# A last layer taken as two passes over all tokens, each with half of its inner width

## The chip, the cores and the metric

The kernel runs on one core of one Trainium2 chip. The metric is the device time of one execution in microseconds (us), as the median of several runs. The core has five engines with their own instruction queues: PE (TensorE, the matmuls; PEld is its weight load), DVE (VectorE), ACT (ScalarE), POOL (GpSimd) and SP (SyncE, which here only issues DMAs). Each engine works its queue in the order of the program; semaphores tie the engines together.

## The reference

Three stages over 3072 tokens of width 512. Inputs are float64 where the kernel converts them (the last layer's weights), the results float32.

```python
attn = softmax(mask(q @ k.T / 8)) @ v              # 4 batches, 8 heads, 768 tokens, window 128, 4 sinks
x    = rows of tokens, heads side by side           # (3072, 512)
# mixture of experts: each token goes to one of 8 experts
e    = argmax(x @ w_gate + modality_bias[modality])
x    = gate_weight * (relu(x @ w1[e]) @ w2[e])      # inner width 1024
# last layer, all tokens
h    = x @ w_in                                     # (3072, 2048)
out  = (h * sigmoid(1.702 * h)) @ w_out             # (3072, 512)
```

## The kernel before

Every float32 product is made of three products of parts: a value is split into a high part (rounded by ScalarE) and what is left (`exact`, line 1189: one ACT copy, then one subtraction on DVE or POOL), and high*high, low*high and high*low are summed in PSUM.

**Attention** (`attention`) is a hand-made schedule of steps; the change leaves it as it is. Tokens are then sorted by expert into slots of 128. Two slots of one expert make a **pair** (256 tokens); an odd last slot of an expert stands **alone**. This run has 12 pairs (the code for pairs 8 and up stands in nested conditions, `more_pairs`, line 1497) and 3 slots alone (`more_alone`, line 1569).

**A pair** (`pair`, line 1460) goes over the 8 chunks `f` of an expert's inner width. For each chunk PE does `first` (line 1248: 12 matmuls of 256 columns, line 1231) and, two chunks behind (`LAG = 2`), `second` (line 1444, `down_pair`: 12 matmuls, line 1246). Between them stands the relu and split of a chunk: ACT makes the high part (line 1254), DVE the low part (line 1257, tile `h`). In chunk 3 PE also transposes the next pair's tokens (line 1202). Beside this run: the gathers of tokens (POOL queue), the stores of the pair's result y with its token numbers to DRAM (SP queue, `columns`, lines 1302 and 1303), and, where a pair's expert differs from the one before, the load of its weights (16 DMAs of 256 KB in two-chunk portions, `others`, line 1435) and a pair later their split (ACT and DVE, 8 times).

**Conversion of the last layer's weights.** Beside the pairs, the last layer's weights come from float64 to float32. The work is cut in **units** (`convert`, `converted`, `stored`, lines 1401 to 1426): a unit is half a chunk of 128 of the last layer's inner width, of `w_in` (even) or of `w_out` (odd), 512 KB in DRAM. There are 32. `cload` (line 1387) brings a unit into one of two buffers `cd`; `convert` is 4 DVE operations (lines 1404 to 1407), `converted` 3 on DVE (lines 1413 to 1415) and a multiplication on POOL (line 1416), `stored` writes the unit away and issues the load of the unit after the next into the buffer that it frees. For the first 16 units `stored` makes the exact parts in place, in the tiles `wb` (two POOL operations, lines 1422 and 1423); for the last 16 there is no place beside the experts' weights, so it stores float32 values to DRAM (`wd`, line 1425, POOL's DMA queue). `units` (line 1489) says which units belong to which pair (`FIRST, SLOPE = 1, 3.2`: some 3.2 a pair), and `pair` spreads their three steps over its 8 chunks, in the program order of DVE: a `convert` whose load has not landed holds up whatever DVE has to do after it.

**The last layer** (from line 1587). The upper half of the weights is loaded from `wd` to the tiles `raw` (8 DMAs, line 1589) and split during the first group into `wa`, which held the experts' weights (`split(f)`, line 1621). Then, for each of 6 groups of 512 tokens, all 16 chunks: `up` (12 matmuls of 512 columns, line 1231), `act` (line 1599: ACT sigmoid, DVE product, ACT high part, DVE low part), and one chunk behind `down` (12 matmuls, line 1238). The next group's tokens are loaded to `cd` (`x2load`, line 1515) and split in the group's last chunk (`msplit`, line 1546: 4 times ACT and DVE). At a group's end `row_out` (line 1605) copies four PSUM tiles out, on DVE and ACT in turns, and POOL scatters their rows to the output (line 1611).

Of the kernel before, what the change touches and what calls it, by code (L numbers as in the profile page):

```python
# [19 lines left out]
NT = S // P            # token tiles of a batch  # L20
T = B * NT             # token tiles
E = 8
DM = H * D
XW = 72                # columns of a head in a row of x: 64 of x, 8 of its logits
KB = P + 4             # a block of keys and the sinks behind it
# [3 lines left out]
# when every kind of the attention's work is issued, in steps of a pair of heads behind its own  # L29
# [5 lines left out]
OPEN = dict(split1=2.908, x0=3.935, split0=4.324, x1=5.361, split2=5.435, split3=6.448, first0=6.794, first1=8.702, split4=13.836)     # steps behind the scores' last at which the first pair's beginnings are  # L35
MORE = 83.434, 0.509, 92.568, 1.089      # the step at which the search for the first pair starts, and its pace; those of its weights


def attention(tc, cst, late, first, spare, q, k, v, wg, xd, then, pick, at_tile, more, opening):
    """Sliding-window attention with sinks; x rows to xd, every tile's logits handed to then().  # L40

    Where the banded path doesn't hold, no rows are written and the logits are zero. The first two
    tiles and the first sinks are in `first`; at_tile holds what else to issue at a tile, `more` at a step.
    `opening` takes turns behind the last scores. `late` holds what the last tiles need longest.
    """
    nc = tc.nc
    ident = cst["ident"]
    with ExitStack() as ctx:
# [12 lines left out]
        def build_back():  # L61
            """Identity and the gate's weights, by head."""
            nc.gpsimd.memset(btw, 0.0)
            nc.gpsimd.tensor_scalar(out=wgs, in0=wgs, scalar1=cst["banded"], scalar2=None, op0=ALU.mult)
            nc.gpsimd.tensor_copy(identr, ident)
            for a in range(2):
                r = slice(64 * a, 64 * a + 64)
                for c in range(4):
                    nc.gpsimd.tensor_copy(btw[r, c, a, 0:64], ident[r, r])
                nc.gpsimd.tensor_copy(btw[r, :, a, 64:72], wgs[r])  # L70

        def build_heads():
            """Rows (part, head, sink) that belong to a head."""
# [11 lines left out]
        # values by head, with nothing beside them; those of a batch's last tile lie across, head beside head  # L85
# [4 lines left out]
        def alone(t):  # L90
            """A batch's last tile, whose own keys are for no other: but the last of all."""
            return t % NT == NT - 1 and t < T - 1

# [5 lines left out]
        # transposed probabilities: of key tile j, the halves are its two query tiles by parity  # L99
# [4 lines left out]
        # what only the scores need  # L104
# [4 lines left out]
        # a batch's first keys lie in the first block of the upper rows and in the second of the lower, with nothing beside them  # L109
# [25 lines left out]
        def load_gate():  # L135
            """The gate's weights of every row's head."""
# [13 lines left out]
        def split_sinks(b):  # L150
            """The sinks' values and logits in exact parts, by head."""
# [52 lines left out]
        def keys(t):  # L204
            """Rows and columns of a tile of keys."""
# [12 lines left out]
        def ksinks():  # L218
            """The sinks' keys behind every block."""
# [10 lines left out]
        def scores(t, c):  # L230
            """A pair of heads, one on the upper rows of the array and one on the lower."""
# [38 lines left out]
        def where(t, kk):  # L270
            """Which half of a bank the probabilities of key tile t - 1 + kk are in: by their places."""
# [51 lines left out]
        def zero(t, g):  # L323
            """The sums of query tile t start from nothing."""
            nc.scalar.activation(out=ops[g][:, :, t % 2, :], in_=zs.unsqueeze(2).broadcast_to([P, 2, P]), func=AF.Copy)

        def pv(t, c):
            """Probabilities times values: key tile t-1 for query tiles t-1, t; at a batch's last tile its own keys too."""
# [13 lines left out]
        def move(t, g):  # L342
            """The lower rows' sums to the other tile's place, which is free by now."""
# [3 lines left out]
        def own(t, g):  # L347
            """Its own keys, for both heads at once: each head's sums are right at one of the two places."""
# [17 lines left out]
        def back(t, g):  # L366
            """Back to tokens by rows, with the logits."""
# [18 lines left out]
        def norm(t, g):  # L386
            """Divided by the sums of the softmax."""
# [39 lines left out]
        # every kind of work: what a unit of it is (a step, half a tile, a tile), and when it is issued, by steps after the unit's own  # L427
# [69 lines left out]
def sink_rows(nc, vs, v, b):  # L497
    """A batch's values of the sinks, on rows (head, sink)."""
# [4 lines left out]
WARM = 13              # products of nothing before the branch, behind the first keys, and at the first steps  # L503
# [4 lines left out]
def warm(tc, cst, spare):  # L508
    """Products of nothing, which have TensorE's clock up by the first that count."""
# [14 lines left out]
def constants(tc, keep, pool, spare, n_sink, window):  # L524
    """Identity, whether the window and the sinks fit the banded path, and what builds its masks."""
    nc = tc.nc
    c = {}
    # the softmax's function, so that its table is there by then
# [9 lines left out]
    # query minus key in the tile's own block, and the key's number in its block  # L538
# [9 lines left out]
    # the banded path holds windows of 1 to P + 1 keys and up to four sinks  # L548
# [19 lines left out]
    def masks():  # L568
# [6 lines left out]
        # kept by the window in the own block and in the one before; kept as a sink in block 0  # L575
# [18 lines left out]
def general(tc, cst, q, k, v, wg, xd):  # L594
    """Attention over all keys, for any window and any number of sinks: x rows to xd, logits beside the bias."""
# [76 lines left out]
NP = 15                # pairs of slots of 128 tokens of one expert that any routing fits in  # L672
NP0 = 8                # pairs that any routing has
NQ = NP + 2
NC = T + E - 1         # slots that any routing fits in
NR = NC - 2            # without the first pair's
ROUND = 1.5 * 2.0 ** 30   # added and taken off again, it rounds to multiples of 128, and its double to those of 256
N0 = 2 * E             # tiles of which some expert has 256 tokens at least
EARLY = 20             # tiles whose experts are picked ahead of the others'


def route_bias(tc, cst, pool, spare, mid, mb):
    """The modality's bias of every token, and the logits of the general path's."""
# [28 lines left out]
def route_constants(tc, cst, pool):  # L712
    """Tiles of the routing's constants, and what fills them."""
# [9 lines left out]
    def fill():  # L723
        G.iota(t["rank"], pattern=[[0, T], [-1, E]], base=E, channel_multiplier=0, **big)       # 8 - e
        G.memset(t["tri"], 1.0)                                                                # q < p
# [4 lines left out]
        G.iota(t["pos"], pattern=[[2 * P, NQ]], base=-2 * P, channel_multiplier=0, **big)       # first places of pairs, behind the first pair  # L730
        G.iota(t["col"], pattern=[[P, 2 * NP - 2]], base=0, channel_multiplier=0, **big)
        G.iota(t["desc"], pattern=[[-P, E]], base=(E - 1) * P, channel_multiplier=0, **big)
        G.iota(t["tok"], pattern=[[P, T]], base=-T * P // 2, channel_multiplier=1, **big)       # the token, from the middle
# [4 lines left out]
def picker(tc, cst, pool):  # L738
    """Every token's expert, the first of the largest logits, as it comes."""
# [25 lines left out]
def opener(tc, cst, pool, perm, raw, gather, load):  # L765
    """The first pair: 256 tokens of the first expert that has as many in the first tiles. What to issue, in turns.

    Its tokens go to the first two columns; the others' routing counts them no more.
# [900 lines left out]
```

## Time and profile before

| | |
|---|---|
| median of 3 runs | 1184.71 us (1183.29 to 1187.19) |
| the profiled execution, first to last instruction (span) | 1182.5 us |
| attention, routing and the first pair | to about 285 us |
| pairs 1 to 11 | about 285 to 596 us |
| slots alone | 596 to 643 us |
| last layer | 643 us to the end |
| PE busy over the span | 93% |
| DVE, ACT, POOL busy | 50%, 38%, 25% |

The page gives no other time for the profiled execution than its span; it lies 2.2 us below the median of the runs. In the page's slices, the busy share of an engine is in tenths, and PEclk is the TensorE clock that was granted, in tenths of 2.4 GHz; its two levels are 1.2 and 2.4 GHz. A wait is put down to the engine or transfer that ended last before it.

### The profile page before, as it was taken

The page shows a single profiled execution, that of the slowest core. Times are in us where ns is not written, and L with a number is a line of the kernel's source. Part 1 is how long each engine was busy: PE and PEld are TensorE (multiplying, and loading weights), DVE is VectorE, ACT ScalarE, POOL GpSimd, SP SyncE. Part 2 cuts the span into 40 slices and gives each one's busy share as a digit, 9 for nine tenths or more (in the row PEclk, how much of TensorE's full clock was granted, in tenths as well). Part 3 has the DMA queues.
Part 4 walks back from the last instruction along what each step waited for, and adds up shares of the span by engine and source line. Part 5 has one row for each costly group of instructions (what it writes and reads, how often), then busy time and mean ns, then how long its engine had stood idle before and what let it go on. Part 6 is the DMA issues. An engine that isn't in the chain of part 4 may idle for free.

```text
span 1182.5 us, 19589 instructions
## 1 busy us (share of the span) xinstructions
PE 1105.4 (93%) x6925; PEld 976.3 (83%) x6925; DVE 591.4 (50%) x1419; ACT 451.3 (38%) x1098; POOL 290.1 (25%) x505
## 2 busy tenths in 40 slices
PE   6999999888999888998778999999999999999996
PEld 5888898788999888988677888888888888888885
DVE  4989898786655777666410533223223223223221
ACT  4999999653222332222121423223223223223221
POOL 5855463452443444323110001001001001001001
PEclk8999999898999898998978999999999999999998
DMA  6598889671778856566676201002002002000000
GB/s 114 102 126 116 112 114 103 97 149 55 111 120 121 222 101 141 118 144 186 175 181 195 49 1 62 10 1 72 1 1 72 1 1 72 1 1 36 1 1 36
DMA packets 164569, 98.07 MB, mean 83 GB/s; under 512 B 117616, under 2 KB 149360, under 8 KB 164432
## 3 DMA queue, kind: packets, MB, share of 16 engines
q1 hardware_dynamic: 158352, 76.75, 36.7%
q0 software_dynamic: 6080, 19.68, 4.9%
q8 instruction: 63, 1.03, 0.4%
q14 instruction: 74, 0.61, 0.2%
HBM read 71.22 MB, written 25.19 MB: 82 GB/s over the span
## 4 chain that ended last, share of the span: by engine, by line
issue 44%; DMA 10%; POOL 2%; PE 2%; DVE 1%; POOLq 0%; DVEq 0%; another core or an unknown queue 0%; ACT 0%; SPq 0%
DMA yb<-y 4%; DMA cd<-in_moe_w_in_dram 2%; DMA cd<-in_moe_w_out_dram 2%; POOL out_dram L1611 1%; DMA wd<-cw 1%; PE pa L1246 1%; DMA raw<-in_moe_w_dram 1%; POOL cw L1416 1%; PE pu L1231 0%; DVE ca L1404 0%; DVE cd L1405 0%; DVE cd L1406 0%; DVE ca L1407 0%; POOLq L1665 0%
## 5 line engine op out<-in xcount | busy, mean ns | idle before, releaser
L1602 DVE TENSOR_TENSOR s<-pu,s 128x512 f32<-128x512 f32 x96 | 66.4, 692 | 318.5 <-ACT s L1601 318.5
L1246 PE MATMUL pa<-h,wah 128*128 128x256 f32 x768 | 164.8, 297 | 30.3 <-DVE h L1257 19.3
L1231 PE MATMUL pu<-xh,wah 128*128 128x256 f32 (+1 forms) x576 | 187.5, 326 | 0.2 <-ACTq L1340 0.2
L1231 PE MATMUL pu<-xh,wal 128*128 128x256 f32 (+1 forms) x576 | 186.1, 323 | 0.5 <-DVEq L1340 0.5
L1231 PE MATMUL pu<-xl,wah 128*128 128x256 f32 (+1 forms) x576 | 185.9, 323 | 0.0
L1601 ACT ACTIVATE s<-pu 128x512 f32<-128x512 f32 x96 | 57.3, 597 | 306.0 <-PE pu L1231 306.0
L1246 PEld LDWEIGHTS pa<-h,wah 128*128 128x128 f32 x768 | 134.0, 203 | 33.2 <-DVE h L1257 21.4
L1611 POOL DMA_INDIRECT out_dram<-xg,oidx x12 | 11.9, 991 | 502.9 <-DVE xg L1610 501.0
L1231 PEld LDWEIGHTS pu<-xh,wal 128*128 128x128 f32 x576 | 112.4, 195 | 8.3 <-DVEq L1340 0.7
L1231 PEld LDWEIGHTS pu<-xh,wah 128*128 128x128 f32 x576 | 112.6, 195 | 8.1 <-ACTq L1340 0.4
L1231 PEld LDWEIGHTS pu<-xl,wah 128*128 128x128 f32 x576 | 112.4, 195 | 7.6
L1254 ACT ACTIVATE h<-pu 128x256 fp32r<-128x256 f32 x96 | 36.8, 383 | 212.3 <-PE pu L1231 196.8
L1246 PE MATMUL pa<-h,wal 128*128 128x256 f32 x384 | 112.6, 293 | 0.0
L268 ACT ACTIVATE pn<-sc,mx 128x260 f32<-128x260 f32 (+1 forms) x192 | 93.9, 492 | 0.3
L1190 ACT ACTIVATE h<-s 128x512 fp32r<-128x512 f32 x96 | 60.7, 633 | 73.4 <-DVE s L1602 73.4
L259 DVE CUSTOM_DVE_ANT_0 sc<-s,m 128x260 f32<-128x260 f32 (+1 forms) x192 | 72.9, 399 | 20.0 <-PE s L251 8.3
L1246 PEld LDWEIGHTS pa<-h,wal 128*128 128x128 f32 x384 | 77.9, 203 | 0.0
L1416 POOL TENSOR_TENSOR cw<-cd 128x512 f32<-128x512 f32 x32 | 37.4, 1169 | 162.8 <-DVE cd L1415 69.4
L1231 PE MATMUL pu<-xh,wbh 128*128 128x512 f32 x192 | 75.8, 395 | 0.8 <-issue 0.8
L1238 PE MATMUL pa<-wbh,h 128*128 128x512 f32 x216 | 76.5, 390 | 0.0
L1238 PE MATMUL pa<-wah,h 128*128 128x512 f32 x216 | 76.4, 390 | 0.0
L1231 PE MATMUL pu<-xl,wbh 128*128 128x512 f32 x192 | 75.5, 393 | 0.0
(349 smaller groups left out, 2522.9 us busy)
## 6 DMA issues: line engine op xcount, KB each, us to landing
raw<-in_moe_w_dram SPq DMA_DIRECT2D x64, 256.0 KB
cd<-in_moe_w_in_dram SPq DMA_DIRECT2D x16, 512.0 KB
cd<-in_moe_w_out_dram SPq DMA_DIRECT2D x16, 512.0 KB
xd<-xe SPq DMA_DIRECT2D x24, 256.0 KB
qn<-in_q_dram SPq DMA_DIRECT2D x22, 256.0 KB
kn<-in_k_dram SPq DMA_DIRECT2D x22, 256.0 KB
vn<-in_v_dram SPq DMA_DIRECT2D x22, 256.0 KB
yb<-y SPq DMA_DIRECT2D x10, 512.0 KB
```

The costliest lines, as they stand in the source:

```text
L259: nc.vector.tensor_tensor_reduce(out=sc[:, :n], in0=ps[:, :n], in1=m[:, :n], scale=1.0, scalar=3.0e38, op0=ALU.add, op1=ALU.min, accum_out=mx)
L268: nc.scalar.activation(out=pn[t][:, h, :n], in_=sc[:, :n], func=AF.Exp, scale=-1.0, bias=mx, accum_out=sums[t][:, h : h + 1])
L1190: A.activation(out=hi, in_=x, func=AF.Copy)
L1231: nc.tensor.matmul(ps[:, 0:n], w[a][:, s], cols(x, b, k), start=(k == 0 and i == 0), stop=(k == 3 and i == 2))
L1238: nc.tensor.matmul(acc, h[a][:, s], w[b][:, 512:], start=(f == 0 and j == 0), stop=(f == last and j == 2))
L1246: nc.tensor.matmul(acc[:, i % 2 * 256 : i % 2 * 256 + 256], wa[f][a][:, s], h[b], start=(f == 0 and i % 2 == 0 and j == 0), stop=(f == CH ...
L1254: A.activation(out=hi, in_=ps, func=AF.Relu)
L1416: G.tensor_tensor(out=cw, in0=lo.bitcast(F32), in1=hi.bitcast(F32), op=ALU.mult)
L1601: A.activation(out=s, in_=ps, func=AF.Sigmoid, scale=1.702)
L1602: V.tensor_tensor(out=s, in0=ps, in1=s, op=ALU.mult)
L1611: s = G.indirect_dma_start(out=out, out_offset=rows(oidx, t), in_=os[i], in_offset=None, bounds_check=T * P - 1, oob_is_err=False)
```

## The change

The last layer is taken in two passes. The first takes all six groups of tokens through the 8 lower chunks of the inner width, with the weights in `wb`, and stores the partial sums of every 128 tokens to DRAM (`yp`, 256 KB each). The second takes all six groups through the 8 upper chunks, with the weights in `wa`, loads the partial sums back, adds them and scatters the rows. So there are 12 turns of 8 chunks where there were 6 groups of 16, and the tokens are loaded and split for each turn. Only the first 16 units are converted beside the pairs, 2 a pair. The other 16 are loaded into seven of the `raw` tiles behind the slots alone and converted in the first pass, from its chunk 3 on: one of the three steps of a unit behind every chunk, two in chunks 1 and 5 of a turn, straight to their exact parts in `wa`. The trip through `wd` and the splits in the first group go. (The full diff also takes comments out, which changes no instruction.)

```diff
-FIRST, SLOPE = 1, 3.2
+FIRST, SLOPE = 1, 2.0
+NU = 16
...
-        m["wd"] = dp.tile([CH, P, F], F32, name="wd")
+        m["yp"] = dp.tile([T * P, DM], F32, name="yp")
...
+    def buffer(u):
+        return cd[u % 2] if u < NU else raw[u % 7]
+
     def cload(u):
-        if u >= 32:
-            return
         f = u // 2
-        d = cd[u % 2].bitcast(U32)
+        d = buffer(u).bitcast(U32)
...
     def stored(u):
         c, s = u // 2, slice(u % 2 * 512, u % 2 * 512 + 512)
-        if c < CH:
-            hi, lo = [x[:, s] for x in wb[c]]
-            G.tensor_scalar(out=hi, in0=cw, scalar1=1.0, scalar2=0.0, op0=ALU.mult, op1=ALU.add)
-            G.tensor_tensor(out=lo, in0=cw, in1=hi.bitcast(F32), op=ALU.subtract)
-        else:
-            nc.gpsimd.dma_start(out=m["wd"][c - CH, :, s], in_=cw)
-        cload(u + 2)
+        hi, lo = [x[:, s] for x in (wb + wa)[c]]
+        G.tensor_scalar(out=hi, in0=cw, scalar1=1.0, scalar2=0.0, op0=ALU.mult, op1=ALU.add)
+        G.tensor_tensor(out=lo, in0=cw, in1=hi.bitcast(F32), op=ALU.subtract)
+        if u + 2 < NU:
+            cload(u + 2)
+        elif NU <= u < 2 * NU - 7:
+            cload(u + 7)
...
     def units(u, to=None):
-        return range(*(min(32, max(0, int(SLOPE * (x - 2) + FIRST))) if x > 1 else 0 for x in (u, u + 1 if to is None else to)))
+        return range(*(min(NU, max(0, int(SLOPE * (x - 2) + FIRST))) if x > 1 else 0 for x in (u, u + 1 if to is None else to)))
...
-    for c in range(CH):
-        nc.sync.dma_start(out=raw[c], in_=m["wd"][c])
-    wm = wb + wa
+    for v in range(NU, NU + 7):
+        cload(v)
+    units = work(range(NU, 2 * NU))
...
-    ss = [tp.tile([P, 512], F32, name=f"s{i}") for i in range(2)]
+    ss = [xs[0], raw[7][:, 0:512]]
...
-    def row_out(g, i):
+    def half_out(g, i):
         t = 4 * g + i
         if i % 2:
             A.activation(out=os[i], in_=pa[i], func=AF.Copy)
         else:
             V.tensor_copy(os[i], pa[i])
+        nc.sync.dma_start(out=m["yp"][t * P : t * P + P, :], in_=os[i])
+
+    def half(g, i):
+        return raw[2 * (g % 2) + i // 2][:, i % 2 * DM : i % 2 * DM + DM]
+
+    def halves_in(g):
+        for j in range(2):
+            r = slice((4 * g + 2 * j) * P, (4 * g + 2 * j + 2) * P)
+            nc.sync.dma_start(out=raw[2 * (g % 2) + j].rearrange("p (i c) -> p i c", i=2), in_=m["yp"][r, :].rearrange("(i p) c -> p i c", p=P))
+
+    def row_out(g, i):
+        t = 4 * g + i
+        V.tensor_tensor(out=os[i], in0=pa[i], in1=half(g, i), op=ALU.add)
         s = G.indirect_dma_start(out=out, out_offset=rows(oidx, t), in_=os[i], in_offset=None, bounds_check=T * P - 1, oob_is_err=False)
...
-    for g in range(NG_):
-        for f in range(16):
-            up(pu[f % 2], wm[f], xt, 512, lambda x, b, k: x[k // 2][b][:, k % 2 * 512 : k % 2 * 512 + 512])
+    turns = [(part, g) for part in range(2) for g in range(NG_)]
+    for n, (part, g) in enumerate(turns):
+        ws = (wb, wa)[part]
+        then = turns[n + 1][1] if n + 1 < len(turns) else None
+        for f in range(CH):
+            up(pu[f % 2], ws[f], xt, 512, lambda x, b, k: x[k // 2][b][:, k % 2 * 512 : k % 2 * 512 + 512])
             act(f)
-            if g == 0 and f < CH:
-                split(f)
-            if f == 15:
-                msplit(g + 1, 0)
-                msplit(g + 1, 1)
+            if then is not None and f == CH - 1:
+                msplit(then, 0)
+                msplit(then, 1)
             if f:
-                down(pa, wm[f - 1], gs[(f - 1) % 2], f - 1, 15)
-            if f == 4 and g + 1 < NG_:
-                x2load(g + 1)
-        msplit(g + 1, 2)
-        msplit(g + 1, 3)
+                down(pa, ws[f - 1], gs[(f - 1) % 2], f - 1, CH - 1)
+            if then is not None and f == 1:
+                x2load(then, n + 1 >= NG_)
+            if part and f == 2:
+                halves_in(g)
+            for _ in range(2 if f % 4 == 1 else 1):
+                if units and CH * n + f >= 3:
+                    fn, v = units.pop(0)
+                    fn(v)
+        if then is not None:
+            msplit(then, 2)
+            msplit(then, 3)
         for i in range(4):
-            down(pa, wm[15], gs[15 % 2], 15, 15, (i,))
-            row_out(g, i)
+            down(pa, ws[CH - 1], gs[(CH - 1) % 2], CH - 1, CH - 1, (i,))
+            (row_out if part else half_out)(g, i)
```

## Rows read from the trace of the kernel before

**Rows 1.** The page: span, and the TensorE clock in 40 equal slices.

```profile
span 1182.5 us, 19589 instructions
...
PEclk8999999898999898998978999999999999999998
```

**Rows 2.** Stretches: A:B and length, each engine's busy us (instructions), clock, DMA share, GB/s.

```profile
463.19:487.08 23.89, 23.89 (x202) 23.89 (x201) 15.95 (x30) 5.97 (x13) 7.06 (x8) 1.00 0.62 129
...
371.05:401.87 30.82, 26.25 (x203) 26.05 (x202) 14.86 (x30) 6.84 (x14) 11.17 (x11) 0.89 1.12 199
401.87:430.75 28.88, 25.66 (x202) 25.25 (x201) 24.58 (x38) 12.81 (x21) 13.28 (x10) 0.94 0.47 116
430.75:463.19 32.44, 27.13 (x207) 26.72 (x206) 26.01 (x47) 7.41 (x15) 16.44 (x15) 0.89 0.67 131
318.15:568.37 250.22, 228.47 (x1806) 226.06 (x1805) 164.71 (x300) 62.90 (x127) 96.00 (x89) 0.95 0.73 144
487.08:568.37 81.29, 75.45 (x602) 74.64 (x601) 49.53 (x94) 17.93 (x39) 25.02 (x26) 0.96 0.67 160
568.37:596.15 27.78, 18.38 (x131) 17.61 (x129) 10.31 (x22) 3.22 (x7) 6.55 (x7) 0.82 0.58 142
642.92:1171.50 528.58, 528.58 (x2304) 433.44 (x2304) 161.92 (x232) 142.43 (x231) 22.04 (x23) 1.00 0.08 26
```

**Rows 3.** Waits of PE from 318.15 to 596.15 us: total us, times, longest.

```profile
PE pa L1246 <- DVE h L1257: 19.3, 10, 4.6
PE pa L1246 <- issue: 5.7, 1, 5.7
PE pa L1246 <- DVEq L1437: 5.3, 2, 3.8
```

**Rows 4.** Waits of DVE in the same stretch.

```profile
DVE ca L1404 <- DMA cd<-in_moe_w_out_dram: 41.8, 11, 11.0
DVE ca L1404 <- DMA cd<-in_moe_w_in_dram: 32.4, 8, 8.2
```

**Rows 5.** Timelines of SP, DVE and PE, one stall: start, us, [idle before <-releaser].

```profile
371.38 0.47 SPq L1395 DMA_DIRECT2D cd<-in_moe_w_out_dram  x1
...
387.42 0.43 DVE L1404 TENSOR_SCALAR ca<-cd 128x512 uint32<-128x512 uint32 x1 [10.15 <-DMA cd<-in_moe_w_out_dram]
...
389.83 0.79 PE L1246 MATMUL pa<-h,wah 128*128 128x256 f32 x2 [4.57 <-DVE h L1257]
```

**Rows 6.** DVE groups by shape, 286 to 596 us: busy us, mean ns of one.

```profile
L1406 DVE TENSOR_SCALAR cd<-cd 128x512 f32<-128x512 int32 x32 | 23.1, 722 | 1.1
...
L1191 DVE TENSOR_TENSOR wal<-raw,wah 128x1024 fp32r<-128x1024 f32 x8 | 12.1, 1550 | 0.0
```

**Rows 7.** Stretch 286 to 596 us, instructions with tile `ca` alone: DVE busy is third.

```profile
286.00:596.00 310.00, 0.00 (x0) 0.00 (x0) 109.44 (x192) 0.00 (x0) 0.94 0.68 141
```

**Rows 8.** Timeline of PE at the last pair's end.

```profile
590.25 0.80 PE L1246 MATMUL pa<-h,wah 128*128 128x256 f32 x2 [2.84 <-DVE h L1257]
```

**Rows 9.** The page's costliest groups: the last layer's `act`.

```profile
L1602 DVE TENSOR_TENSOR s<-pu,s 128x512 f32<-128x512 f32 x96 | 66.4, 692 | 318.5 <-ACT s L1601 318.5
...
L1601 ACT ACTIVATE s<-pu 128x512 f32<-128x512 f32 x96 | 57.3, 597 | 306.0 <-PE pu L1231 306.0
...
L1190 ACT ACTIVATE h<-s 128x512 fp32r<-128x512 f32 x96 | 60.7, 633 | 73.4 <-DVE s L1602 73.4
```

**Rows 10.** DVE groups by shape, 643 us to the end.

```profile
L1191 DVE TENSOR_TENSOR xl<-cd,xh 128x512 fp32r<-128x512 f32 x20 | 12.5, 684 | 0.0
L1191 DVE TENSOR_TENSOR wal<-raw,wah 128x1024 fp32r<-128x1024 f32 x8 | 9.8, 1225 | 2.1 <-ACT wah L1190 1.8 <-DMA oidx<-tb 0.3
```

**Rows 11.** POOL groups by shape, 318.15 to 596 us.

```profile
L1416 POOL TENSOR_TENSOR cw<-cd 128x512 f32<-128x512 f32 x30 | 35.3, 1178 | 150.7 <-DVE cd L1415 60.4 <-DVE ca L1404 34.3 <-issue 23.0
...
L1423 POOL TENSOR_TENSOR wbl<-cw,wbh 128x512 fp32r<-128x512 f32 x14 | 22.0, 1568 | 1.2
L1422 POOL TENSOR_SCALAR wbh<-cw 128x512 fp32r<-128x512 f32 x14 | 11.7, 836 | 1.2
```

More of the change, by code (lines that the diff above doesn't have):

```diff
@@ L1346, in layers @@
     cd, wb, xs = [], [], []
-    c3 = ExitStack()
     def flag(row, i, engines):
@@ L1372, in left3 @@
         wb.extend(parts(pool("wb", side="right"), "wb", 0, CH))
-        tp = pool("moe", c3)
+        tp = pool("moe")
         ca = tp.tile([P, 512], U32, name="ca")
@@ L1397, in halves @@
     def halves(u):
-        d = cd[u % 2].bitcast(U32).rearrange("p (c w) -> p c w", w=2)
+        d = buffer(u).bitcast(U32).rearrange("p (c w) -> p c w", w=2)
         return d[:, :, 0], d[:, :, 1]
@@ L1513, in layers, with x2load @@
     oidx = keep.tile([P, T], I32, name="oidx")
-    def x2load(g):
+    def x2load(g, index=False):
         nm, a = ("b", 512 * g - 256) if g else ("a", 0)
@@ L1519, in x2load @@
             nc.sync.dma_start(out=x.rearrange("p (k c) -> p k c", k=2), in_=m["y" + nm][2 * i : 2 * i + 2, :, a : a + 512].rearrange("k p c -> p k c"))
-        nc.sync.dma_start(out=oidx[:, 4 * g : 4 * g + 4], in_=m["t" + nm][a : a + 512].rearrange("(t p) o -> p (t o)", p=P))
+        if index:
+            nc.sync.dma_start(out=oidx[:, 4 * g : 4 * g + 4], in_=m["t" + nm][a : a + 512].rearrange("(t p) o -> p (t o)", p=P))
     def first_alone(s, f):
@@ L1546, in msplit @@
     def msplit(g, k):
-        if g >= NG_:
-            return
         r = slice(k % 2 * 512, k % 2 * 512 + 512)
@@ L1584, in layers @@
     more_alone(0)
-    c3.close()
-    for c in range(CH):
-        nc.sync.dma_start(out=raw[c], in_=m["wd"][c])
-    wm = wb + wa
+    for v in range(NU, NU + 7):
+        cload(v)
+    units = work(range(NU, 2 * NU))
     pa.append(us[2])
```

## The prediction

> **What bounds the kernel now.** I read the page's clock slices first: TensorE is granted its full 2.4 GHz through the last layer and dips to 1.2 GHz for part of the time between about 350 us and the last layer [rows 1]. The stretches say why. The last layer runs its 2304 matmuls in 528.58 us with PE busy in all of it, 229 ns each: PE bounds it and nothing else shows. Among the pairs, the cleanest interval from one transposition to the next takes 23.89 us at full clock, while others with the same 200 matmuls (a few records more or less) take 28.88, 30.82 and 32.44 us at 0.89 to 0.94 of the clock [rows 2]. Nine such intervals lie in 318.15 to 568.37 us: 250.22 us, against 9 x 23.89 = 215.0, and 0.6 for a slot's extra transposes. So **34.6 us are lost among the pairs**, and some 12 more after 568.37, where 131 matmuls at the clean pace (23.89 / 202 = 118 ns) would take 15.5 of 27.78 us.
>
> The waits name the cause. PE waited for DVE's low part of the relu (line 1257) 10 times for 19.3 us and twice behind DVE's branch for 5.3 us [rows 3]. DVE was not overloaded: it stood 41.8 + 32.4 = 74.2 us in 19 waits at the first operation of a unit, for the float64 load [rows 4]. One stall in full: SP issues a load at 371.38 us, DVE reaches the unit 10.15 us before 387.42 and stands there; the low part queued behind it comes late, and PE stands 4.57 us [rows 5]. That interval is 6.9 us too long [rows 2], since PE comes out of the wait at the lower clock: about 1.5 us lost for 1 us of wait.
>
> **What the change takes from the pairs.** A unit costs DVE (109.44 + 23.1) / 32 = 4.14 us [rows 6, 7]. Pairs now carry 2 instead of 3.2, so DVE is relieved of 1.2 x 4.14 = 5.0 us a pair; the pair with eight weight splits, DVE busy 24.58 of 28.88 us [rows 2], comes to 19.6, below the clean 23.89.
>
> Relief of DVE matters less than the time a load gets. With 2 units a pair, six steps stand behind chunks 0, 1, 2, 4, 5, 6. A load goes out behind `stored(u)` and is wanted at `convert(u+2)`, six chunks on: 6/8 x 23.89 = 17.9 us. In the stall above, the slowest kind (DMA share 1.12 [rows 2]), the load took at most 387.42 - 371.38 = 16.0 us, and was wanted after 5.9 [rows 5]. 16.0 is under 17.9, and PE has two chunks of slack (LAG) on top. Unit 15 falls to pair 9; pairs 10 and 11 carry no unit and have no such wait at all. SP issues the remaining loads in the same places; POOL's 16 stores to `wd` go. How much of the 34.6 us is left can't be seen before: at best 0, as in the clean interval (also three units); at worst all but the three intervals from 487.08 us, whose loss is 81.29 - 71.67 = 9.6 [rows 2], so 25.0. I take 3, near the clean row, since 17.9 exceeds the worst load time seen. **Gain 31.6** (9.6 to 34.6).
>
> At the last pair's end PE waits 5.7 us for nothing the profile shows, at the jump out of the nested conditions [rows 3], and then 2.84 us for the low part behind unit 31's load [rows 8]. The first I leave; the second goes with the unit. **Gain 2.8** (0, if the jump gets longer, to 8.5, if both go). The slots alone carry no unit: no change.
>
> **What it adds to the last layer.** Matmuls: the same 2304. The eight `wd` loads and eight splits (DVE 9.8 us [rows 10]) go; no wait of PE stood on them, so nothing is gained. Added:
> - 16 units, 16 x 4.14 = 66 us of DVE, in 46 chunks of 12 x 229 ns x 2 = 5.5 us. A turn of 44 us carries 10 steps, 3.33 units, 13.8 us, beside `act`'s 8 x 2 x 0.69 = 11.0 [rows 9], four `xl` of 0.68 = 2.7 [rows 10] and two copies, bounded by the same 0.69 each: 29 of 44 us. In a chunk, `act` needs 597 + 692 + 633 + 692 ns = 2.6 us plus its hand-overs [rows 9], and its result is wanted 5.5 us after `up`: the 2.5 us or so of a convert behind it stay hidden, and so do the 4.1 of two steps, since 1.4 + 4.1 = 5.5 a chunk and the neighbours hold less.
> - POOL: 1178 + 836 + 1568 ns a unit [rows 11], 57 us in 250, with nothing queued behind that is due.
> - Turn ends, 11 inside the layer instead of 5. There `act` has only one `down`, 2.75 us, and the low part half a microsecond more; the four `msplit` (2.7 us of DVE), a convert in two of the ends and the copies come before the next `act`. Where a convert stands there, DVE ends the last `xl` some 8.0 us behind the last `up` (2.6 + 2.7 + 2.5 and hand-overs), and the matmul that reads it, the 36th from there, starts at 35 x 229 ns = 8.0. So the five ends with units have no slack left: the price is 0 to one POOL operation, 1.57 us [rows 11], times 1.5 for the clock, 5 times, 0 to 12 us. I take **2**, near 0, as only two ends have a convert there. Ends of the second pass have four additions (PSUM and SBUF, as L1602, 0.69 us) for the copies, and no unit: 0.
> - SP: seven loads at the layer's start, nine more behind POOL's multiplications, six more `x2load`, 24 stores and 12 loads of partial sums. A turn moves at most 1 MB of tokens, 1 MB of sums and 1.7 MB of weights: 3.7 MB at the 199 GB/s seen [rows 2] is 19 us of 44. `x2load`, issued after chunk 1, stands behind at most a multiplication's wait and is wanted in chunk 7, some 33 us on. Hidden; without that cover it would cost the 16.0 us of the slowest load, once a turn.
> - The tail: one addition for the last copy, 0.1 us, in the 2.
>
> Weighed on the side: L1191 on two SBUF tiles takes 1225 ns with POOL still [rows 10] and 1550 beside POOL's units [rows 6], so `act`'s low part will be slower in the first pass. The Trainium skill, "SBUF — State Buffer", section "Who interferes with whom", says that a DVE instruction with two SBUF inputs and a GpSimd one that reads SBUF block each other for a whole instruction. By that rule each of the five ends could meet one block, 7.8 us instead of my 2, and the total would be 1158, inside the forecast's range; by the row's mean, 0.3 us an instruction, it stays at 2.
>
> **Sum:** 31.6 + 2.8 - 2 = 32.4 us off the profiled 1182.5, 1150.1. The runs' median is 2.2 higher: **1152.3 us**.
>
> **The rivals.**
> 1. *The loads still come late where expert weights are loaded and split.* The six intervals up to 487.08 us keep their 25.0. For: the DMA share there reaches 1.12 [rows 2]. Against: 17.9 us of lead. Gain 9.6 + 2.8 - 2 = 10.4: 1174.3 us.
> 2. *Slower: DVE at the turn ends.* Eleven ends in which DVE comes a unit's 4.14 us late behind `msplit` and copies, less 0.4 of slack, times 1.5: 62 us, so 1184.7 - 34.4 + 62 = 1212 us. It decides from 34.4 / 11 / 1.5 = 2.1 us of lateness an end. For: an end has next to no slack. Against: six ends have no unit, and before, with PE busy without a break over five ends [rows 2], `msplit` and copies already stood there.
> 3. *The stall moves with the units.* 16 of 32 units leave the pairs with half of the loss, 17.3 us, and cost PE as much in the first pass, where DVE works in the same order: 1184.7 - 2.8 = 1182 us. For: the same 4.14 us a unit. Against: `act` of a whole 512-column chunk gives DVE 5.5 us, and seven load buffers take the load's wait away.
>
> **How the numbers follow.** Chances: forecast 0.76, rival 1 0.13, rival 2 0.06, rival 3 0.05. About 0.3%, 3.6 us, can be told from no change. Faster: 0.76 + 0.13 = 0.89; within: rival 3, 0.05; slower: rival 2, 0.06. Range: the low end takes all 34.6, 5.7 at the last pair's end and no cost, 1184.7 - 40.3 = 1144. The high end takes half the loss as left (17.3), 2.8, and 8 of the 12 us at the ends: gain 12.1, 1172.6, rounded to 1173. Rival 1's 1174 and the slower ones lie just or far outside.
>
> **What would show it.** Right: intervals of 24 to 25 us among the pairs at a clock of 0.98 or more; DVE's waits at line 1404 nearly gone in the pairs and absent in pairs 10 and 11; the last layer still some 529 us with PE busy throughout; the 5.7 us at the jump still there. Wrong: DVE waits for `cd` loads of several us in the pairs with weight loads (rival 1); gaps of PE at the turn ends, waiting for `xl`, `h` or `g` (rival 2), or in the middle of the turns of the first pass (rival 3), with clock slices under 0.95 behind 640 us.

## The result and the profile after

The changed kernel takes **1147.61 us** (median of 4 runs, 1147.54 to 1147.92) against 1185.14 (4 runs): ratio 0.9689, 95% interval 0.9669 to 0.971. Forecast were 1152.3 us in a range of 1144 to 1173. Its profiled execution spans 1145.9 us, 36.6 less than before's 1182.5 [rows 1]. The span and the clock slices on its page:

```profile
span 1145.9 us, 19741 instructions
...
PEclk9999999999999999999988999999999999999999
```

The clock's dips among the pairs are gone but for one stretch at 0.94; the slots alone still stand at 0.89. The stretches (columns: stretch, length, busy time and instructions of each engine, clock, DMA share, GB/s) answer to [rows 2]:

```profile
317.18:543.18 226.00, 218.34 (x1807) 217.29 (x1806) 104.39 (x205) 62.88 (x127) 62.67 (x62) 0.99 0.63 113
344.32:368.22 23.90, 23.90 (x203) 23.90 (x202) 11.87 (x25) 5.97 (x13) 7.96 (x9) 1.00 0.87 111
392.12:417.90 25.78, 24.15 (x202) 23.95 (x201) 18.00 (x27) 12.94 (x21) 6.82 (x6) 1.00 0.68 164
417.90:447.57 29.67, 26.31 (x207) 25.91 (x206) 16.11 (x32) 7.29 (x15) 11.81 (x12) 0.94 0.64 103
543.18:562.39 19.21, 15.64 (x130) 15.27 (x128) 3.67 (x7) 3.21 (x7) 2.98 (x3) 1.00 0.49 88
562.39:607.72 45.33, 33.51 (x264) 32.51 (x265) 2.77 (x4) 10.19 (x26) 3.98 (x5) 0.89 0.63 166
607.72:1136.30 528.58, 528.57 (x2304) 433.15 (x2304) 239.01 (x383) 148.08 (x248) 71.37 (x71) 1.00 0.22 71
```

The first row is the nine intervals among the pairs, 226.00 us against 250.22: 24.2 gained. Six of the nine take 23.90; the last two single rows and the first interval (27.14) hold what is still lost, 226.00 - 215.6 = 10.4 us. The last pair's end takes 19.21 instead of 27.78 (8.6 gained), the slots alone 1.4 less. The last layer takes 528.58 us, **the same to a hundredth**, now in two passes with the conversions beside the first. With 1.0 ahead of the pairs and 1.4 behind the last matmul these are the 36.6.

The waits of PE from 317.18 to 562.39 us, then DVE's wait for a `cd` load from 317 to 1146, then SP's wait from 399 to 410 (columns: engine, tile, line, what it waited for, us, times, longest):

```profile
PE pa L1247 <- issue: 5.4, 4, 2.7
PE pt L1203 <- ACT xg L1212: 2.6, 1, 2.6
PE pa L1247 <- DVE h L1258: 2.4, 2, 1.6
```

```profile
DVE ca L1405 <- DMA cd<-in_moe_w_out_dram: 5.8, 1, 5.8
```

```profile
SPq L1396 <- DMA raw<-in_moe_w_dram: 8.8, 1, 8.8
```

Against [rows 3, 4]: PE's waits for the low part fell from 19.3 us to 2.4, DVE's for a unit's load from 74.2 us to 5.8 there. That one late load stood 8.8 us on SP behind expert weights in flight, though POOL's last read of its buffer had ended at 390.2 us and SP's issue before it had come at 399.6; so it lost its lead. PE's 2.6 us are for a gather of POOL's (`xg`) queued behind the units' work. They don't hang on the late load alone: in the run four below, where DVE waits for no load, PE waits 3.5 us there, and in no_units, without units, not at all.

### The profile page after: what moved, and what is told of

Same layout as the page of the kernel before. It is cut to its first block, busy times and chain, and to the rows that moved or that the text cites. A ratio compares the mean times of both kernels' runs of the same rounds, so it can differ in the third digit from the quotient of the medians.

```text
span 1145.9 us, 19741 instructions
## 1 busy us (share of the span) xinstructions
PE 1089.3 (95%) x6925; PEld 962.1 (84%) x6925; DVE 598.9 (52%) x1459; ACT 456.2 (40%) x1114; POOL 302.8 (26%) x521
## 4 chain that ended last, share of the span: by engine, by line
PE 56%; issue 4%; DMA 2%; POOL 0%; ACT 0%; POOLq 0%; DVE 0%; another core or an unknown queue 0%; ACTq 0%; DVEq 0%
PE pu L1232 26%; PE pa L1239 16%; PE pu L1239 5%; PE pa L1247 5%; PE pa L1540 1%; DMA tb<-perm 1%; PE pu L1531 1%; DMA xg<-xd,perm 1%; PE pt L1203 1%; POOL out_dram L1626 0%; ACT xg L1212 0%; POOLq L1688 0%; DVE xs L1602 0%; DVE y L1313 0%; ACT xs L1601 0%
## 5 line engine op out<-in xcount | busy, mean ns | idle before, releaser
L1247 PE MATMUL pa<-h,wah 128*128 128x256 f32 x768 | 155.7, 286 | 7.3 <-issue 5.0
L1247 PEld LDWEIGHTS pa<-h,wah 128*128 128x128 f32 x768 | 127.7, 194 | 6.9 <-issue 4.1
L1247 PE MATMUL pa<-h,wal 128*128 128x256 f32 x384 | 109.3, 285 | 0.4 <-issue 0.4
L1602 DVE TENSOR_TENSOR xs<-pu,xs 128x512 f32<-128x512 f32 x48 | 33.2, 691 | 131.9 <-ACT xs L1601 130.5
L1258 DVE SCALAR_TENSOR_TENSOR h<-pu,h 128x256 fp32r<-128x256 f32 x96 | 40.3, 422 | 113.6 <-ACTq L1439 58.2
L1601 ACT ACTIVATE xs<-pu 128x512 f32<-128x512 f32 x48 | 28.7, 598 | 159.5 <-PE pu L1232 159.5
L1602 DVE TENSOR_TENSOR raw<-pu,raw 128x512 f32<-128x512 f32 x48 | 33.2, 691 | 109.3 <-ACT raw L1601 108.0
L1601 ACT ACTIVATE raw<-pu 128x512 f32<-128x512 f32 x48 | 28.7, 598 | 135.2 <-PE pu L1232 133.7
L1247 PEld LDWEIGHTS pa<-h,wal 128*128 128x128 f32 x384 | 74.4, 194 | 1.9 <-issue 1.9
```

The lines of the kernel that those rows point to most:

```text
L1247: nc.tensor.matmul(acc[:, i % 2 * 256 : i % 2 * 256 + 256], wa[f][a][:, s], h[b], start=(f == 0 and i % 2 == 0 and j == 0), stop=(f == CH ...
L1258: V.scalar_tensor_tensor(out=lo, in0=ps, scalar=0.0, in1=hi.bitcast(F32), op0=ALU.max, op1=ALU.subtract)
L1601: A.activation(out=s, in_=ps, func=AF.Sigmoid, scale=1.702)
L1602: V.tensor_tensor(out=s, in0=ps, in1=s, op=ALU.mult)
```

## The experiments

The chips differ: the kernel before took 1185 to 1196 us on those used, so kernels are compared by their ratio to it; the fourth column is that ratio times the 1185.14 us of the first result, the scale on which times were expected. "Lost" is the length of the nine intervals less the 215.6 us of nine clean ones (the prediction's working). It was 34.6 in the kernel before and 10.4 in the changed one; other executions of the same pairs lost 10.9, 13.9 and 15.5 (late_burst, after_again, crowd), so **differences under some 5 us of it are not told apart**. For the kernel before the spread is wider: short_else executes the same pairs as before and lost 43.2, which is 8.6 more.

| run | ratio to before | 95% interval | us on that scale | nine intervals, us | lost, us |
|---|---|---|---|---|---|
| after_again | 0.9684 | 0.9662 to 0.9705 | 1148 | 229.54 | 13.9 |
| short_lead | 0.9887 | 0.9864 to 0.991 | 1172 | 252.65 | 37.1 |
| dense | 0.9811 | 0.9789 to 0.9833 | 1163 | 240.89 | 25.3 |
| dense_four | 0.9689 | 0.9665 to 0.9712 | 1148 | 228.59 | 13.0 |
| four | 0.9695 | 0.9664 to 0.9726 | 1149 | 229.78 | 14.2 |
| pool_loads | 0.9766 | 0.9744 to 0.9789 | 1157 | 230.50 | 14.9 |
| no_units | 0.9704 | 0.9675 to 0.9733 | 1150 | 228.02 | 12.4 |
| no_branch | 0.971 | 0.969 to 0.973 | 1151 | 230.74 | 15.1 |
| crowd | 1.0083 | 1.0059 to 1.0106 | 1195 | 231.14 | 15.5 |
| end_free | 1.0134 | 1.01 to 1.0169 | 1201 | 274.38 | 58.8 |
| short_else | 1.0006 | 0.9982 to 1.003 | 1186 | 258.76 | 43.2 |
| late_burst | 0.9696 | 0.9662 to 0.9731 | 1149 | 226.48 | 10.9 |

### Lead of the load, or load of DVE

**short_lead**: one float64 load ahead instead of two, all else as changed.

```diff
-        if u + 2 < NU:
-            cload(u + 2)
+        if u + 1 < NU:
+            cload(u + 1)
```

(and only `cload(0)` at the start)

> Units, buffers and order stay those of the changed kernel; only each float64 load among the pairs is issued one unit later, two chunks (6.0 us) ahead of its conversion in place of six (17.9 us). Lead theory (the stalls of before came from loads issued 5.9 us ahead): DVE stands again at the first operation of nearly every unit, 40 us or more in all; before lost 34.6 us over some 29 loads, 1.2 us a load, so 16 loads lose 19 us against the 10.4 left now: 1155 to 1165 us. DVE theory (the stalls came from DVE carrying 3.2 units a pair): two units a pair as now, 1147 to 1150 us.

**dense**: the changed kernel at the old pace.

```diff
-FIRST, SLOPE = 1, 2.0
+FIRST, SLOPE = 1, 3.2
```

> The 16 units of the pairs at the old pace, 3.2 a pair, done by pair 6; two buffers, so a load has some 10 us of lead or less. Lead theory and DVE theory agree: the intervals with units lose as before (17.0 us over the four from 318 to 431 us, against 5.2 there now), while the later ones, without units, lose nothing (5.2 us now): 1150 to 1160 us. A third theory, that only the number of units counts: 1148 us. The run is the base for the next one.

**dense_four**: dense, with four buffers (the two more lie where the last chunk of `wb` comes later; units 14 and 15 use the first two again).

```diff
-        return cd[u % 2] if u < NU else raw[u % 7]
+        return (cd + cx)[u % 4 if u < NU - 2 else u % 2] if u < NU else raw[u % 7]
...
-        if u + 2 < NU:
-            cload(u + 2)
+        if u + 4 < NU - 2:
+            cload(u + 4)
+        elif NU - 4 <= u < NU - 2:
+            cload(u + 2)
```

> As the dense kernel, 3.2 units a pair, but with four buffers for the float64 halves, so that a load is issued some 26 us ahead of its conversion. Lead theory: DVE's waits for loads are nearly gone and the time falls to that of the changed kernel or some us below, 1140 to 1149 us. DVE theory: the intervals with units stay as long as in the dense kernel, 1150 to 1160 us.

DVE's waits for loads from 316 to 594 us, then the stretch: the nine intervals of short_lead, the first four of dense (11 of its 16 units), and the nine of dense_four, in this order:

```profile
DVE ca L1404 <- DMA cd<-in_moe_w_in_dram: 58.7, 7, 12.2
DVE ca L1404 <- DMA cd<-in_moe_w_out_dram: 6.5, 1, 6.5
```

```profile
316.99:569.64 252.65, 225.33 (x1807) 223.60 (x1805) 105.62 (x205) 62.86 (x127) 64.65 (x62) 0.95 0.59 103
```

```profile
DVE ca L1405 <- DMA cd<-in_moe_w_out_dram: 20.2, 4, 10.6
DVE ca L1405 <- DMA cd<-in_moe_w_in_dram: 14.5, 3, 9.5
```

```profile
320.61:438.77 118.16, 103.71 (x802) 102.61 (x801) 73.74 (x131) 31.59 (x60) 48.43 (x43) 0.91 0.82 133
```

```profile
DVE ca L1408 <- DMA cd<-in_moe_w_out_dram: 4.3, 1, 4.3
```

```profile
318.02:546.61 228.59, 220.84 (x1806) 220.11 (x1805) 109.81 (x203) 62.98 (x127) 66.71 (x61) 0.98 0.63 108
```

The three settle it. With **two units a pair but a short lead**, DVE no busier (105.6 us in 252.65) than in the changed kernel (104.4 in 226.00), the whole loss is back: 65 us of DVE's waiting, 37.1 us lost, more than the 19 I expected and as much as before's (34.6, and 43.2 in short_else). With **3.2 units a pair** and two buffers, the four intervals that carry 11 of the 16 lose 118.16 - 95.6 = 22.6 us. The same units at the same pace with **four buffers** lose 13.0 in all nine, with DVE as busy as in dense (109.8 us against 110.0): the level of the changed kernel, and its ratio. So the lead sets this loss and DVE's load does not. What I called the DVE theory falls. My sizes were too low: by estimate a late load costs (37.1 - 12.4) / 16 = 1.5 us on top of what no_units loses below, where I had 1.2.

### What is left among the pairs

**four**: the changed kernel with dense_four's buffers and 2.2 units a pair. **pool_loads**: its loads issued by POOL.

```diff
+        q = nc.gpsimd if u < NU else nc.sync
...
-            nc.sync.dma_start(out=d, in_=w_out[f * P : f * P + P, :])
+            q.dma_start(out=d, in_=w_out[f * P : f * P + P, :])
```

> The changed kernel with four buffers for the float64 halves of the pairs and 2.2 units a pair: a load is issued some 36 us ahead of its conversion, so SP may hold it 8.8 us and it still comes in time. Lead theory: DVE waits for no load, the intervals but the one with the stall at a branch take 23.9 us, 5 us less than the changed kernel: ratio to before 0.964 to 0.966. Rival (the late load was an accident of one place, or the traffic of earlier loads costs as much): 0.968 to 0.971, as the changed kernel or above.

> The changed kernel with the float64 loads of the pairs issued by POOL instead of SP. Theory: the one late load left (wait of 5.8 us on DVE, for a load that SP issued 8.8 us late behind expert weights in flight) and the gather behind it go, worth 1.9 + 5.8 us of the intervals at 414 to 447 us: 1139 to 1143 us. Rival: the load is late for the traffic and not for the queue, or POOL's own issuing holds its multiplications: 1146 to 1150 us.

**no_units**: no conversion among the pairs; POOL writes a constant's parts in place of the weights', so the output is not the reference's.

```diff
-        cload(0)
-        cload(1)
+        V.memset(cw, 0.5)
...
+        if u < NU:
+            return
```

(the last two lines in both `convert` and `converted`; `stored` issues no load there)

> The changed kernel with the conversion among the pairs left out (no float64 loads there, no work of DVE's; POOL stores constants as the first half's parts), so the first half's weights are not the reference's. The floor of the pairs. Theory: the late load and the gather behind it go (5.2 us), the stall at a branch near 323 us stays, with no unit near it: intervals of 27.1 and 8 times 23.9 us, ratio 0.963 to 0.966. Rival (that stall is the units' too): all nine at 23.9 us, 0.960 to 0.963.

None of the three gained. In four and in pool_loads DVE waits for no load at all among the pairs, and they still lose 14.2 and 14.9. pool_loads is 0.008 slower than the changed kernel, which neither of my two theories had. Against dense_four on the same chip its profile is 8.6 us longer: 2.6 ahead of the nine intervals, 1.9 in them, 2.9 at the last pair's end and in the slots alone, 1.2 behind; the cause was not followed up. In no_units the loads and DVE's work are gone, yet 12.4 us are lost. Its first five intervals, then the same five of after_again:

```profile
322.23:349.69 27.46, 24.55 (x203) 24.09 (x202) 5.38 (x11) 5.97 (x13) 5.82 (x6) 1.00 0.57 59
349.69:379.91 30.22, 26.66 (x203) 26.28 (x202) 5.29 (x11) 5.86 (x13) 5.81 (x6) 0.89 0.62 53
379.91:406.25 26.34, 24.33 (x203) 23.97 (x202) 5.38 (x11) 6.84 (x14) 5.83 (x6) 1.00 1.13 144
406.25:430.16 23.91, 23.91 (x203) 23.91 (x201) 16.08 (x19) 12.79 (x21) 7.41 (x6) 1.00 0.43 109
430.16:454.60 24.44, 24.44 (x207) 24.36 (x206) 5.38 (x11) 7.29 (x15) 6.96 (x7) 1.00 0.26 55
```

```profile
320.47:348.86 28.39, 25.52 (x203) 25.31 (x201) 11.97 (x25) 5.98 (x13) 7.98 (x9) 0.94 0.75 94
348.86:373.57 24.71, 24.15 (x203) 23.95 (x202) 11.87 (x25) 5.98 (x13) 7.98 (x9) 1.00 0.90 108
373.57:398.01 24.44, 24.18 (x203) 24.01 (x202) 11.87 (x25) 6.84 (x14) 7.99 (x9) 1.00 0.93 148
398.01:422.87 24.86, 24.14 (x202) 23.94 (x201) 17.98 (x27) 12.96 (x21) 6.82 (x6) 1.00 0.71 174
422.87:454.36 31.49, 27.30 (x207) 26.90 (x206) 16.12 (x32) 7.30 (x15) 11.85 (x12) 0.89 0.63 97
```

The late load and the gather behind it did go (the chips of the two runs differ): the last two take 48.35 us instead of 56.35. But the first three take 84.0 instead of 77.5, with DVE nearly idle: in each of the three ACT stands once for 6.4 to 8.1 us (for two of these waits the profile names PE, whose matmuls of that chunk had ended 4 us or more before). In all, the units now cost the pairs nothing that can be told apart (12.4 lost without them, 10.4 to 15.5 with them), though the last two intervals alone are 8.0 us shorter without them. **Even without units this stage does not come down to the clean rows.**

**no_branch** asks whether the branch around the expert splits makes that floor.

```diff
-        with tc.If(new[u] != 0):
+        if u == 5:
```

> The changed kernel with the branch around the expert weights' splits resolved for this input: the splits stand in pair 5 without a branch, and in no other pair, so ACT and DVE have no branch inside a pair up to the eighth. Theory (what is left among the pairs, 10.4 us, is mostly instruction code that arrives late at a branch): the stall near 323 us goes, nine intervals in 216 to 222 us, ratio 0.003 to 0.010 under the changed kernel's of this job. Rival (code arrives late in straight runs too, or the stall is another's): as the changed kernel, within 0.002.

**after_again** is its base, the changed kernel unaltered.

> The changed kernel once more, as a base for its neighbours here: ratio 0.967 to 0.971. Its nine intervals among the pairs took 226.0 us in its first profile and 231.1 in the kernel that crowds the first pass, whose pairs are the same code; if such differences are the chip's or the execution's, this run lies anywhere between 225 and 232.

The branch theory falls: 0.971 against 0.9684, and the stalls stand in straight code now. ACT's waits of no_branch from 321 to 390 us, then ACT's two relus around the first stall:

```profile
ACT h L1255 <- remote: 22.2, 3, 7.6
```

```profile
324.11 0.38 ACT L1255 ACTIVATE h<-pu 128x256 fp32r<-128x256 f32 x1 [0.79 <-PE pu L1232]
...
332.09 0.38 ACT L1255 ACTIVATE h<-pu 128x256 fp32r<-128x256 f32 x1 [7.60 <-remote]
```

ACT stands 7.6 us for something that is no engine's of this core ("remote"), DVE behind it, PE two chunks later. The DMA queues of no_branch from 331.2 to 332.1 us show one instruction packet; from 324.5 to 331.2, the seven microseconds before, there is none:

```profile
q14 instruction: 1, 0.01, 2.9%
```

That reads as ACT's code arriving at the end of the wait, behind the gathers' and loads' data. It fits this first wait, but no run shows it: one without any gather in flight there was not made. The other two of the three waits don't fit. From 353.2 to 360.9 us the only instruction packet is one of 16 KB that begins at 360.36 and ends at 361.38, after ACT has gone on; from 380.7 to 387.7 there is none. What ACT waits for **stays open**.

### The last pair's end

**end_free**: the kernel before with no unit in its last pair.

```diff
-FIRST, SLOPE = 1, 3.2
+FIRST, SLOPE = 1, 3.6
```

> The kernel before with 3.6 units a pair in place of 3.2, so that the last pair has none; all else stays. If the unit of the last pair made both waits there (the jump's 5.7 us and the low part's 2.8), the stretch from the last pair's transposition to the first slot alone falls from 27.8 to 19 or 20 us. If the jump's wait belongs to the jump, it stays and the stretch takes 24 to 26 us. The pairs themselves lose a little more than before, for the denser units: 5 us or so. In all 0.996 to 1.002 of before.

**short_else**: the kernel before without code that this input never enters.

```diff
-            for fn, v in work(units(u, NP)) if u < NP else ():
-                fn(v)
```

> The kernel before without the code of left-over units in the branches not taken behind the pairs; for this input nothing that is executed changes. Theory for the last pair's end: the jump's wait (5.7 us before, 7.4 with fewer units there, 2.7 now) is paid for the code that the jumps pass over, 30 units of it before and 4 now: it falls to 3 or 4 us, and the stretch from the last pair's transposition to the first slot alone from 27.8 to 24 to 26 us, the low part's 2.8 staying. Rival (it is the unit in the last pair, or chance): 27 us or more. In all 0.995 to 1.000 of before.

**late_burst**: the changed kernel with two loads ahead of the jump.

```diff
+            if u == 11 and f == 6:
+                for i in range(2):
+                    V.tensor_copy(cw[:, i : i + 1], cd[i][:, 0:1])
+                    nc.sync.dma_start(out=cd[i].bitcast(U32), in_=w_out[i * P : i * P + P, :])
```

> The changed kernel with two loads of 512 KB that nobody reads, issued in the last pair when the low part of its seventh chunk is done, some 1.5 us before TensorE's code for the jump is fetched; before, the load of unit 31 was issued there. Theory (PE's wait at the jump is the transfer of its code, two packets of 16 KB, and that stands behind data in flight): the gap at the jump, 3.0 to 4.1 us in the changed kernel's two profiles, grows to 5 to 8 us, and the stretch from the last pair's transposition to the first slot alone, 19.2 and 22.6 us there, to 23 to 27; ratio 0.970 to 0.976. Rival (the wait is something else's): gap 3 to 4.1 us, stretch at most 22.6, ratio 0.967 to 0.970.

PE's first matmul behind the jump in after, in end_free, and in short_else with the matmul that waits for the low part behind it (columns: start, length, instruction, and in brackets the idle time before it and what ended it):

```profile
558.44 0.36 PE L1247 MATMUL pa<-h,wah 128*128 128x256 f32 x1 [2.73 <-issue]
```

```profile
613.59 0.55 PE L1246 MATMUL pa<-h,wah 128*128 128x256 f32 x1 [7.41 <-issue]
```

```profile
598.29 0.55 PE L1246 MATMUL pa<-h,wah 128*128 128x256 f32 x1 [5.02 <-issue]
...
601.82 0.58 PE L1246 MATMUL pa<-h,wah 128*128 128x256 f32 x1 [2.77 <-DVE h L1257]
```

Without a unit in the last pair the low part's wait is gone and the jump's is not (7.41 us): the two have different causes, and only the first is the units'. Its stretch takes 25.4 us (593.65 to 619.07). In the pairs, end_free also shows where a still denser pace leads: 58.8 us lost, 1.3% slower in all, far beyond the 5 us I gave it. Code that is passed over makes no difference either: short_else's jump costs 5.02 us, as before.

late_burst tests the next idea, that data in flight delays the code PE jumps to, and missed its mark. Its two loads and the first matmul behind the jump:

```profile
558.13 2.54 SPq L1473 DMA_DIRECT2D cd<-in_moe_w_out_dram  x2
...
561.99 0.36 PE L1247 MATMUL pa<-h,wah 128*128 128x256 f32 x1 [2.17 <-issue]
```

The two 16 KB instruction packets began at 557.50 and 558.47 us, so the loads came too late to stand in front of the first. The jump's wait stayed small (2.17 us, below even the rival's 3 to 4.1), but the theory's condition was not met. The wait is 2.2 to 4.5 us in the changed kernel and its variants and 5.0 to 7.4 in the kernel before and its own. The traces narrow down why. In all 14 the first matmul behind the jump starts 4.4 to 5.3 us after the first of the two packets begins. What differs is where that beginning lies against PE's work: in the changed kernel and its variants 0.3 to 2.3 us before PE falls idle (553.92 against 555.71 us in after), in before, short_else and end_free 0.5, 0.6 and 2.9 us behind it (609.04 against 606.18 in end_free). So the wait is long where the packets begin late, not where they take longer; what sets their beginning **stays open**.

### How much the first pass can hide

**crowd**: four steps of units a chunk.

```diff
-            for _ in range(2 if f % 4 == 1 else 1):
+            for _ in range(4):
```

> The changed kernel with four steps of units a chunk in the first pass in place of one or two: 16 units in 12 chunks, turn end included. DVE then needs 1.33 x 4.14 = 5.5 us for units and 1.4 for act in a chunk of 5.5. Theory (the first pass is free for its slack, and no more): DVE is 1.4 us late a chunk, PE stands 12 x 1.4 = 17 us and loses up to 1.5 times that: last layer 545 to 555 us in place of 528.6, ratio 0.983 to 0.992. Rival: DVE has slack that I did not count, or waits for POOL and the loads thin the units out by themselves: last layer within 3 us of 528.6, ratio 0.969 to 0.971.

Its last layer, PE's waits in it, and ACT's from 621.9 to 800 us:

```profile
621.90:1197.60 575.70, 544.54 (x2304) 440.34 (x2304) 261.31 (x383) 147.38 (x248) 76.02 (x71) 0.97 0.20 65
```

```profile
PE pa L1239 <- ACT h L1191: 25.9, 8, 7.4
PE pu L1232 <- DVE xl L1192: 3.6, 2, 3.1
```

```profile
ACT h L1191 <- DVE raw L1602: 46.8, 12, 8.8
ACT h L1191 <- DVE xs L1602: 38.5, 12, 8.3
```

The layer grows by 575.70 - 528.58 = 47.1 us, more than the 16 to 26 I expected, and the change with it is slower than no change at all. ACT waits for DVE's product of `act`, queued behind units; PE waits for ACT's `g` and `h`. The slack of the first pass is real and ends somewhere between 1.25 and 4 steps a chunk.

## Why the prediction was right

**The main step held.** Most of the loss among the pairs came from loads issued too late, and 17.9 us of lead removes that part: short_lead gives the loss back and dense_four takes it away at the old pace. That relief of DVE matters less was right too; by dense_four it matters not at all within the resolution.

**Terms of the sum.** Four were mis-sized, and that they nearly cancel is luck: 32.4 us forecast, 36.6 measured.
- Pairs: 31.6 forecast, 24.2 measured. The step that failed is "near the clean row": I put all 34.6 us down to loads and left 3. Without any unit these intervals still lose 12.4, in places where ACT stands 6.4 to 8.1 us and not DVE. The profile of before could not show me this: PE's waits in its nine intervals are all put down to DVE, and none of ACT's from 286 to 600 us to "remote". short_else, which executes the same pairs, has one such wait of 7.9 us. How much of before's 34.6 was this second cause is not shown. One late load also came (5.8 us), where SP held the issue for 8.8 us; I had counted lead from the place of the code, not from when its queue can issue.
- Last pair's end: 2.8 forecast, 8.6 measured. The low part's 2.8 went with the unit, as end_free confirms. The jump's wait, which I left standing, halved; the sign "the 5.7 us at the jump still there" failed. That the gain meets my upper bound of 8.5 is chance: the two waits gave 2.84 + 3.0 us, and PE at the full clock through this end (1.00 in its row, 0.82 before) worked 15.64 us instead of 18.38. In after_again the same end takes 22.59 us at a clock of 0.85, a gain of 5.2.
- Last layer: a cost of 2 forecast, 0.0 measured. The turn ends with a convert cost nothing. (The working spreads the 16 units over 46 chunks; 48 steps, ten a turn, end after 39, and the trace has the last convert at 827.48 us, in the sixth turn. The load of a turn, which the sum rests on, was counted rightly.)
- Not in the sum: 3.8 us of small gains ahead of the pairs, in the slots alone and behind the last matmul, where the last scatter's issue to the end took 6.9 us instead of 8.2. None was tested.

**The 1.5 us lost for 1 us of wait** held: in crowd PE waited 32.0 us in all and its last layer grew by 47.1, 1.47 for 1.

**The rivals.** Rival 1 (late loads beside the expert weights) showed once, 5.8 us, by SP's queue. Rivals 2 and 3 did not happen, and crowd shows that they were no empty threat: the same work packed into 12 chunks costs 47 us.

**The rule weighed on the side.** DVE's low part in the first pass (607.72 to 872 us), then the same line in the second:

```profile
L1192 DVE TENSOR_TENSOR h<-xs,h 128x512 fp32r<-128x512 f32 x24 | 20.2, 840 | 16.8 <-ACT h L1191 16.8
```

```profile
L1192 DVE TENSOR_TENSOR h<-xs,h 128x512 fp32r<-128x512 f32 x24 | 16.6, 692 | 16.8 <-ACT h L1191 16.8
```

Beside POOL's units it takes 840 ns on average instead of 692, and PE, busy 528.57 of 528.58 us, paid none of it. The Trainium skill, "SBUF — State Buffer", section "Who interferes with whom", has the two engines block each other on such operands. The 0.15 us agrees with that rule in sign.

## What to carry to other kernels

For a load that feeds work hidden beside a busy engine, compare its lead in microseconds (buffers ahead times the spacing of the work, less what its queue holds back) with the slowest load seen under traffic; more buffers or sparser work both cure it here, and the busy share of the engine that stood waiting says little. Before putting a stage's whole loss down to one wait, ask what the stage takes with that work left out: here it still lost 12.4 us, where I had put the whole 34.6 down to loads. Slack beside a full engine is worth filling, but measure its end: the same 16 units cost nothing at 1.25 steps a chunk and 47 us at four.

## What the runs showed of the hardware that I had not expected

An engine can stand 7 to 8 us in straight code while the profile names nothing of its own core that it waits for (ACT, three times and 22.2 us in no_branch). Instruction packets of 8 and 16 KB share the DMA engines with the data; one came at the end of the first of these waits, none in the third. Behind the jump, PE's first matmul started 4.4 to 5.3 us after the first packet began, in all 14 traces. And a DMA issue can stand 8.8 us on SP behind other transfers that are in flight, with its buffer free; six other traces with such loads on SP have one held there for 8.9 to 14.1 us.
